# Fused local and coarse attention with a soft mixture of experts on one core: scores of both heads of a pair in one product, new layouts and a new order

## The chip, the cores and the metric

The kernel runs on one core of one Trainium2 chip. The metric is device time in microseconds (us) of one execution. Before the change three runs took 379.61, 382.04 and 382.05 us, median 382.04. The profile is of one more execution, which took 383.51 us, with a span of 381.7 us from its first to its last instruction.

## What is computed

Attention with 8 batches, 8 heads, 576 positions and 64 features a head, followed by a soft mixture of 8 experts with 4 slots each. All is 32-bit.

```python
q_d, k_d, v_d = (mean of 4 neighbouring positions of q, k, v)   # 144 positions
out_up = repeat(softmax(0.125 * q_d @ k_d.T) @ v_d, 4)
mask = abs(pos[:, None] - pos[None, :]) < 4                     # a band 7 wide
out_local = softmax(where(mask, 0.125 * q @ k.T, -1e9)) @ v
x = (out_up + out_local), as (4608 tokens, 512)
logits = x @ phi                                                # (4608, 32)
slot_input = softmax(logits, over tokens).T @ x                 # (32, 512)
slot_out[e] = relu(slot_input[e] @ w1[e]) @ w2[e]               # 512 -> 1024 -> 512
out = softmax(logits, over slots) @ slot_out
```

## The kernel before

x is never formed. The program holds instead, for each head, the product of v with that head's rows of phi, and gets the logits from attention weights times that product; the slot inputs come the same way, with the attention weights applied to the token weights first.

**Halves and steps.** The attention runs over 16 halves: a half is two pairs of heads (r = 0, 1) of one batch, four heads (k = 0 to 3). Two halves make a step, one batch. Two heads of a pair lie on partitions 0 to 63 and 64 to 127 (`h2`). The operations of a half, by their names in the order table: `lq` loads a pair's queries, keys and values in one DMA (888 KB); `pa`, `pb` (GpSimd, lines 145 and 151) add neighbours for the coarse means; `lv` loads values in another layout (640 KB); `sl` (line 173) makes the local scores, 24 queries by 30 keys a product, above a mask that two bf16 products (line 163) write first; `slm` to `sln` are their softmax; `ptt`, `pte` transpose the weights; `vf` (line 238) is v times phi; `sd`, `sr` (lines 275, 285) are the coarse scores (128 queries, and the last 16 of 144), `sde` their exponentials (ScalarE), `sdn` the division (GpSimd, lines 325 to 328); `td` transposes them; `loc` (372) and `plg` (381 to 388) add both parts to the logits of the step in PSUM. After the second half the step's softmax over tokens follows (`pl`, `lts`, `mx` to `dx`, `dtt`), and then for both halves `es` (405) and `ed` (415 to 422), which apply the attention weights to the token weights, `ede` to `ett`, and `so` (452), the product with v. The halves overlap: `es` of a step stands among the `sl` of the next.

**How the products lie in the array.** TensorE products name a tile of the array by `tile_position`. A score product takes 64 rows and a strip of 32 columns, so that eight of them lie beside each other; `es` takes tiles of 24 rows by 32 columns on the diagonal, four beside each other; `loc`, `plg`, `ed` and `so` take all 128 rows and a strip of 32 columns, four beside each other. The trace shows a 32-bit product as two weight loads and two matmuls (so 96 products of a half's `sl` are 192 of each); a transpose or a bf16 product is one of each.

**What sets the order.** Within the attention, every engine's order is written by hand in the string ORDER: all engines take their instructions in that order, SP its DMAs too. Loads of expert weights stand in it as `w:n` (512 KB each). The first 27 of 64 (NW) go into their own buffers during the attention. 24 more (NW2) go into memory that attention tiles give back, each as soon as its place is free, and the last 13 into places of used weights.

**After the attention** (the tail) come the slot inputs, the first layer (`a<-wt,sits`, line 639), the second (666), and the outputs (691 to 699), 24 of them, in an order by hand for TensorE and SP.

Of the kernel before, what the change touches and what calls it, by code (L numbers as in the profile page):

```python
# [11 lines left out]
F32 = mybir.dt.float32  # L12
# [30 lines left out]
NW = 27  # L43
NW2 = 24
NP_, ND, NQK, NV, NWK = 4, 4, 4, 2, 2

# [9 lines left out]
def body(ctx, tc, qkv_, vk, phi, w1, w2, cst, cstb, out):  # L56
# [27 lines left out]
    with ExitStack() as att:  # L84
        ld = att.enter_context(tc.tile_pool(name="ld", bufs=NQK))
        lv = att.enter_context(tc.tile_pool(name="lv", bufs=NV))
        per = att.enter_context(tc.tile_pool(name="per", bufs=1))
        wk = att.enter_context(tc.tile_pool(name="wk", bufs=NWK))
        w1k = att.enter_context(tc.tile_pool(name="w1k", bufs=1))
# [10 lines left out]
        ets = [per.tile([P, 4, 160], F32, name=f"et{i}") for i in range(2)]  # L100
        lgs = [per.tile([P, 152], F32, name=f"lg{i}") for i in range(2)]
        dts = [per.tile([P, 152], F32, name=f"d{i}") for i in range(1)]
# [9 lines left out]

        halves = [{} for _ in range(2 * B)]
        steps = [{"started": set()} for _ in range(B)]
        qts = {}

        def load_qk(i):
            b, pr = divmod(i, NPR)
            qts[i] = ld.tile([P, VO + KP], F32, name="qkv")
            sp.dma_start(out=qts[i], in_=qkv_[b, pr])  # L120

        def ops_half(h):
# [4 lines left out]
            e, pd, pk, pdr = es[h % NP_], pds[h % ND], pks[h % ND], pdrs[h % ND]  # L127
# [8 lines left out]
            for r in range(2):  # L136
                @at(f"lq{r}")
                def _(r=r):
                    load_qk(q[r])

                @at(f"pa{r}")
                def _(r=r):
                    t4 = qts[q[r]][:, 0:VO - 4].rearrange("p (t f) -> p t f", f=4)
                    t = hd[f"tmp{r}"] = w1k.tile([P, QP + 1 + SD, 2], F32, name="tmp")
                    pool.tensor_tensor(out=t, in0=t4[:, :, 0:2], in1=t4[:, :, 2:4], op=ALU.add)  # L145

                @at(f"pb{r}")
                def _(r=r):
                    t = hd[f"tmp{r}"]
                    hd[f"qd{r}"] = w1k.tile([P, QP + 1 + SD], F32, name=f"qd{r}")  # L150
                    pool.tensor_tensor(out=hd[f"qd{r}"], in0=t[:, :, 0], in1=t[:, :, 1], op=ALU.add)  # L151
# [72 lines left out]
            def _():  # L224
                hd["pt"] = wk.tile([P, NC, NG, QB], F32, name="pt")
# [5 lines left out]
            def _():  # L231
                vf = hd["vf"] = bank2("vf").rearrange("p a n -> p (a n)")
                for c0, c1 in ((0, 512), (512, KP)):
                    for r in range(2):
                        for h2 in range(2):
                            k = 2 * h2 + r
                            o = slice(64 * h2, 64 * h2 + 64)
                            pe.matmul(vf[32 * k:32 * k + 32, c0:c1], lhsT=phs[o, 2 * hf + r, :],  # L238
                                      rhs=qts[q[r]][o, VO + c0:VO + c1], start=True, stop=True,
                                      tile_position=(64 * h2, 32 * k), skip_group_check=True)  # L240
# [7 lines left out]
            def _():  # L248
                dve.tensor_reduce(out=vdps[h % 2][:, 0:SD], in_=hd["vf"][:, 4:4 + S].rearrange("p (t f) -> p t f", f=4),  # L249
# [13 lines left out]
            def _():  # L263
                hd["vr"] = wk.tile([P, SLOTS], F32, name="vr")
                dve.transpose(out=hd["vr"], in_=vdps[h % 2][:, P:160])


            @at("sd")
            def _():
                sd = hd["sd"] = bank2("sd")  # L270
                for r in range(2):
                    for h2 in range(2):
                        o = slice(64 * h2, 64 * h2 + 64)
                        qd = hd[f"qd{r}"]
                        pe.matmul(sd[:, h2, SD * r:SD * r + SD],  # L275
                                  lhsT=qd[o, 0:P], rhs=qd[o, QP + 1:], start=True, stop=True, tile_position=(64 * h2, 0), skip_group_check=True)

            @at("sr")
            def _():
                for r in range(2):  # L280
                    for h2 in range(2):
                        o = slice(64 * h2, 64 * h2 + 64)
                        qd = hd[f"qd{r}"]
                        k = 2 * h2 + r
                        pe.matmul(hd["sd"][32 * k:32 * k + 32, 0, 2 * SD:3 * SD],  # L285
                                  lhsT=qd[o, QP - 32:QP], rhs=qd[o, QP + 1:], start=True, stop=True, tile_position=(64 * h2, 32 * k), skip_group_check=True)
# [590 lines left out]
```

## Time and profile before

| | |
|---|---|
| Median of three runs | 382.04 us |
| Profiled execution, its span | 383.51 us, 381.7 us |
| TensorE matmuls: busy, share, number | 273.6 us, 72%, 9098 |
| TensorE weight loads: number | 9098 |
| VectorE, ScalarE, GpSimd busy | 147.7, 104.9, 160.0 us |
| Mean granted TensorE clock | 0.783 of 2.4 GHz |
| DMA | 84.25 MB, mean 221 GB/s |

How to read it: busy is the time in which an engine had an instruction under way. A wait is the idle time of an engine before an instruction, with what ended it; "issue" stands where the engine waited for nothing that the profile can name. The profile also counts DMA queues: q1 carries the program's own loads and stores, q8 carries instructions to the engines, in packets of 16 KB. An instruction is 64 bytes, so a packet holds 256; TensorE's two times 9098 instructions are 1.16 MB, which is what q8 moved. The text calls such a packet a block.

### The profile page before, as it was taken

The numbers are of one execution on the slowest core, as the hardware profiler recorded it, in microseconds if no ns is written. First come the engines' busy times: TensorE is split into PE (matmuls) and PEld (weight loads), VectorE is DVE, ScalarE is ACT, GpSimd is POOL, SyncE is SP. The second block draws the span as 40 slices with busy tenths as digits, with TensorE's granted clock in tenths as the row PEclk, the third lists the DMA queues.
The fourth block names the chain that finished last, engine by engine and source line by source line (L and its number), as shares of the span: only waits on it lengthen the run. The fifth ranks groups of instructions, "written<-read, shape, count | busy, mean of one in ns | idle before, by whom it ended". The sixth has DMA issues, their size and how long they took to land.

```text
span 381.7 us, 19650 instructions
## 1 busy us (share of the span) xinstructions
PE 273.6 (72%) x9098; PEld 199.8 (52%) x9098; DVE 147.7 (39%) x329; ACT 104.9 (27%) x333; POOL 160.0 (42%) x270
## 2 busy tenths in 40 slices
PE   0775695968487647785875688668795775999983
PEld 0534363845375537663763575447574664235552
DVE  1462632344334433452361534443480344001552
ACT  1222233222304140423141414140441411010442
POOL 3754827271627263636272625463742253100000
PEclk9986867596858885986596958875997855799997
DMA  7897536055903690289045900760272159999997
GB/s 271 324 330 300 191 149 271 6 214 206 379 8 115 247 413 32 99 327 377 6 136 184 373 6 10 258 261 5 72 299 109 52 203 320 411 409 409 385 371 289
DMA packets 20098, 84.25 MB, mean 221 GB/s; under 512 B 2224, under 2 KB 2608, under 8 KB 20016
## 3 DMA queue, kind: packets, MB, share of 16 engines
q1 hardware_dynamic: 20016, 82.99, 56.6%
q8 instruction: 71, 1.16, 1.2%
q14 instruction: 11, 0.09, 0.1%
HBM read 73.55 MB, written 9.44 MB: 217 GB/s over the span
## 4 chain that ended last, share of the span: by engine, by line
PE 69%; issue 23%; DVE 3%; DMA 2%; POOL 1%; ACT 0%; SPq 0%; ACTq 0%
PE ep L405 11%; PE sl L173 9%; PE vf L238 6%; PE a L639 4%; PE pt L220 4%; PE a L666 4%; PE so L452 4%; PE o L691 3%; PE sd L275 3%; PE td L335 2%; PE l L372 2%; PE ep L422 2%; DMA qkv<-qkv 2%; PE ep L415 2%; PE sl L163 2%
## 5 line engine op out<-in xcount | busy, mean ns | idle before, releaser
L173 PE MATMUL sl<-qkv 64*24 64x30 f32 x3072 | 34.2, 207 | 57.6 <-issue 51.3
L173 PEld LDWEIGHTS sl<-qkv 64*24 64x24 f32 x3072 | 29.8, 106 | 66.1 <-issue 58.9
L405 PE MATMUL ep<-e,dt 24*32 24x60 f32 x1536 | 44.2, 300 | 10.3 <-issue 9.2
L405 PEld LDWEIGHTS ep<-e,dt 24*32 24x32 f32 x1536 | 39.1, 166 | 12.9 <-issue 10.4
L183 DVE TENSOR_REDUCE nm<-sl 128x24 f32<-128x720 f32 x16 | 14.5, 908 | 79.8 <-PE sl L173 79.7
L145 POOL TENSOR_TENSOR tmp<-qkv 128x594 f32<-128x594 f32 x32 | 37.7, 1178 | 12.8 <-DMA qkv<-qkv 11.9
L195 ACT ACTIVATE e<-e 128x768 f32<-128x768 f32 x16 | 13.5, 846 | 69.2 <-DVE e L187 69.2
L325 POOL TENSOR_TENSOR pdr<-pdr,dd 128x144 f32<-128x144 f32 x16 | 6.8, 427 | 60.5 <-DVE dd L320 60.5
L309 ACT ACTIVATE xd<-sd,nd 128x144 f32<-128x144 f32 x64 | 23.5, 380 | 26.2 <-POOL nd L301 26.2
L440 POOL TENSOR_TENSOR et<-et,ed 128x576 f32<-128x576 f32 x16 | 19.2, 1212 | 26.6 <-ACT et L435 23.7
L238 PE MATMUL vf<-qkv,phs 64*32 64x512 f32 (+1 forms) x256 | 26.0, 520 | 1.4 <-issue 1.4
L151 POOL TENSOR_TENSOR qd<-tmp 128x297 f32<-128x297 f32 x32 | 21.8, 683 | 8.7 <-PE sd L285 7.6
L212 POOL TENSOR_TENSOR e<-e,den 128x720 f32<-128x720 f32 x16 | 22.5, 1406 | 2.5 <-DVE den L208 1.3
L452 PE MATMUL so<-v,ett 128*32 128x64 f32 x640 | 16.4, 260 | 8.8 <-issue 8.2
L227 ACT COPY pt<-pt 128x576 f32<-128x576 f32 x16 | 10.3, 646 | 45.0 <-PE pt L220 45.0
L187 DVE TENSOR_TENSOR e<-sl,nm 128x768 f32<-128x768 f32 x16 | 15.2, 952 | 15.2 <-PE ep L405 14.9
L249 DVE TENSOR_REDUCE vdp<-vf 128x144 f32<-128x576 f32 x16 | 12.1, 757 | 23.2 <-PE vf L238 23.1
L238 PEld LDWEIGHTS vf<-qkv,phs 64*32 64x32 f32 x256 | 9.1, 129 | 18.8 <-issue 18.5
L452 PEld LDWEIGHTS so<-v,ett 128*32 128x32 f32 x640 | 13.0, 133 | 10.5 <-issue 8.6
L639 PE MATMUL a<-wt,sits 128*32 128x512 f32 x128 | 16.8, 672 | 1.3 <-DVE sits L606 1.3
L220 PE MATMUL pt<-cs,e 128*128 128x128 f32 x96 | 17.6, 333 | 0.0
L445 DVE STREAM_TRANSPOSE ett<-et 128x640 f32<-128x640 f32 x16 | 13.0, 815 | 9.7 <-POOL et L440 9.6
(122 smaller groups left out, 536.6 us busy)
## 6 DMA issues: line engine op xcount, KB each, us to landing
wt<-w SPq DMA_DIRECT2D x64, 512.0 KB, 9.0
qkv<-qkv SPq DMA_DIRECT2D x32, 888.0 KB, 7.3
v<-vk SPq DMA_DIRECT2D x16, 640.0 KB, 4.4
out<-o SPq DMA_DIRECT2D x16, 432.0 KB, 4.2
out<-o SPq DMA_DIRECT2D x8, 288.0 KB, 4.6
cs<-cst SPq DMA_DIRECT2D x1, 208.0 KB, 2.4
cb<-cstb SPq DMA_DIRECT2D x1, 128.0 KB, 2.2
phs<-phi SPq DMA_DIRECT2D x1, 64.0 KB, 2.1
```

Source lines behind the costliest of these rows:

```text
L145: pool.tensor_tensor(out=t, in0=t4[:, :, 0:2], in1=t4[:, :, 2:4], op=ALU.add)
L151: pool.tensor_tensor(out=hd[f"qd{r}"], in0=t[:, :, 0], in1=t[:, :, 1], op=ALU.add)
L173: pe.matmul(s5[32 * g:32 * g + QB, h2, c, r, 1:31], lhsT=t[o, q0:q0 + QB], rhs=t[o, KO + s0 + 1:KO + s0 + 31], start=False, stop=True, til ...
L212: pool.tensor_tensor(out=e3[:, :, 1:31], in0=e3[:, :, 1:31], in1=hd["den"].unsqueeze(2).broadcast_to([P, 24, 30]), op=ALU.mult)
L220: pe.transpose(pt.rearrange("p a n -> p (a n)")[:, o:o + P], e[:, c].rearrange("p k u -> p (k u)"), ident)
L238: pe.matmul(vf[32 * k:32 * k + 32, c0:c1], lhsT=phs[o, 2 * hf + r, :], rhs=qts[q[r]][o, VO + c0:VO + c1], start=True, stop=True, tile_posi ...
L309: act.activation(xd[:, k], hd["sd"][:, k // 2, SD * (k % 2):SD * (k % 2) + SD], AF.Exp, scale=SCALE_D, bias=nd[:, k:k + 1], accum_out=dd[: ...
L405: pe.matmul(ep[32 * g:32 * g + 32, 2 * h2:2 * h2 + 2, QB * c + 1:QB * c + 31], lhsT=st["dt"][o, c, :], rhs=e[o, c, 2 * h2:2 * h2 + 2, 1:31 ...
L440: pool.tensor_tensor(out=x4, in0=x4, in1=hd["ed"].unsqueeze(3).broadcast_to([P, 4, XG, 4]), op=ALU.add)
L452: pe.matmul(so[32 * k:32 * k + 32, :], lhsT=hd["ett"][:, k, kb, :], rhs=hd["v"][:, kb, k, :], start=kb == 0, stop=kb == NK - 1, tile_posit ...
L639: pe.matmul(hp[o:o + 32, :], lhsT=sits[:, kc, :], rhs=wt[(1, e + x, kc)][:, 512 * f:512 * f + 512], start=kc == 0, stop=kc == NPR - 1, til ...
L666: pe.matmul(soq[u][32 * g:32 * g + 32, :], lhsT=hts[e // 4][:, e % 4, 2 * g + f, :], rhs=w[:, g], start=(e, f) == (0, 0), stop=(e, f) == ( ...
```

## The change

The scores of both heads of a pair become one product. Queries lie with the two heads' features interleaved over 128 partitions; the keys of head 0 go to even partitions of one block of columns, those of head 1 to odd partitions of a second block, and the other half of each block is zero (set once; the three buffers `qk0` to `qk2` are kept). One product of 128 rows then gives 24 queries by 2 x 30 keys. The coarse scores do the same (128 x 2 x 144), and their sums of neighbours now also run over the zero blocks. phi lies as a block-diagonal matrix, so that one product of 64 columns gives both heads of a pair. `es` multiplies tiles of 64 by 64, with a token weight matrix that is masked to be block-diagonal (`dtm`, GpSimd). `plg` takes all four groups of positions in one product. The logits are completed in PSUM: `lrp` adds the coarse part, each column four times, by a product; the sum stays in PSUM and is read from there, and is copied (`ktr`) for the end, where it is transposed at once.

`sdn` moves from GpSimd to ScalarE (five multiplications of 128x144), half of the `pb` from GpSimd to VectorE. A pair's loads become four DMAs (304, two of 146 and 292 KB, the same bytes in sum). Three buffers for queries and keys and two for values take the place of four for all; 31 expert weight tiles are loaded during the attention, not 27, and 19 go into given-back memory, not 24. Memory pools stand in another order, and ORDER is new.

```diff
-NW = 27
-NW2 = 24
-NP_, ND, NQK, NV, NWK = 4, 4, 4, 2, 2
+NW = 31
+NW2 = 19
+NQK, NVT, NP_, ND, NV, NE_ = 3, 2, 4, 4, 2, 1
...
-                    load_qk(q[r])
+                    t = qkt[q[r]] = qks[n % NQK]
+                    sp.dma_start(out=t[:, 0:QW], in_=qt[b, pr])
+                    for h2 in range(2):
+                        sp.dma_start(out=t[h2::2, QW + KP * h2:QW + KP * h2 + KP], in_=kt[b, pr, h2])
+
+                @at(f"lt{r}")
+                def _(r=r):
+                    hd[f"vt{r}"] = lt_.tile([P, KP], F32, name="vt")
+                    sp.dma_start(out=hd[f"vt{r}"], in_=vt[b, 2 * hf + r])
...
-                    t = hd[f"tmp{r}"] = w1k.tile([P, QP + 1 + SD, 2], F32, name="tmp")
-                    pool.tensor_tensor(out=t, in0=t4[:, :, 0:2], in1=t4[:, :, 2:4], op=ALU.add)
+                    t = hd[f"tmp{r}"] = w0.tile([P, 2, QK // 4], F32, name="tmp")
+                    pool.tensor_tensor(out=t.rearrange("p f t -> p t f"), in0=t4[:, :, 0:2], in1=t4[:, :, 2:4],
+                                       op=ALU.add)
...
-                    pool.tensor_tensor(out=hd[f"qd{r}"], in0=t[:, :, 0], in1=t[:, :, 1], op=ALU.add)
+                    (dve if r else pool).tensor_tensor(out=hd[f"qd{r}"], in0=t[:, 0], in1=t[:, 1], op=ALU.add)
...
-                            for h2 in range(2):
-                                o = slice(64 * h2, 64 * h2 + 64)
-                                pe.matmul(s5[32 * g:32 * g + QB, h2, c, r, 1:31], lhsT=t[o, q0:q0 + QB],
-                                          rhs=t[o, KO + s0 + 1:KO + s0 + 31], start=False, stop=True,
-                                          tile_position=(64 * h2, 32 * g), skip_group_check=True)
+                            pe.matmul(s5[32 * g:32 * g + QB, r, c, :, 1:31], lhsT=t[:, q0:q0 + QB],
+                                      rhs=kk[:, :, s0 + 1:s0 + 31], start=False, stop=True,
+                                      tile_position=(0, 32 * g), skip_group_check=True)
...
-                        for h2 in range(2):
-                            k = 2 * h2 + r
-                            o = slice(64 * h2, 64 * h2 + 64)
-                            pe.matmul(vf[32 * k:32 * k + 32, c0:c1], lhsT=phs[o, 2 * hf + r, :],
+                        pe.matmul(vf[64 * r:64 * r + 64, c0:c1], lhsT=phs[:, 2 * hf + r, :], rhs=hd[f"vt{r}"][:, c0:c1],
...
+                    o = win(hd["sd"], 552 * r, 184, 2, SD)
+                    pe.matmul(o, lhsT=hd[f"qd{r}"][:, 0:P], rhs=kd(r), start=True, stop=True, skip_group_check=True)
...
+                for j in (2, 0, 1, 3, 4):
+                    o = pdr[:, 0:SD] if j == 2 else pd[:, j - j // 3, 0:SD]
+                    act.mul(o, o, hd["dd"][:, j:j + 1])
+
+            @at("pkc")
+            def _():
+                pool.tensor_copy(out=pk[:, :, 0:16], in_=pd[:, :, P:SD])
...
+                for c in range(NC):
+                    for r in range(2):
+                        for w in range(2):
+                            o = slice(64 * w, 64 * w + 64)
+                            x = ep[o, r, 0:2 * KW].rearrange("p (h n) -> p h n", h=2)[:, :, QB * c + 1:QB * c + 31]
+                            pe.matmul(x, lhsT=dtb[o, c, :], rhs=e[o, c, 2 * r:2 * r + 2, 1:31], start=c == 0, stop=True,
+                                      tile_position=(64 * w, 64 * w), skip_group_check=True)
...
+            @at("lrp")
+            def _():
+                for g in range(NG):
+                    pe.matmul(st["l"][32 * g:32 * g + 32, 0:TG].rearrange("p (x f) -> p x f", f=4), lhsT=i32,
...
+                pool.tensor_tensor(out=dtb.rearrange("p c (x s) -> p c x s", x=2),
```

Two places show what stands where. First TensorE, where the token weights of the second step are used: from a half's scores on. A name such as e_93 is one of the four buffers of a half's local weights. Before:

```order
L163 MATMUL sl<-cb 128x384
L173 MATMUL sl<-qkv 24x30 x96
L405 MATMUL ep<-e_93,dt 32x2x30 x48
L544 MATMUL drp<-cs,dpx 128x32
L405 MATMUL ep<-e_94,dt 32x2x30 x48
L415 MATMUL ep<-pd_97,dpt 32x2x36 x3
```

After the change, at the same kind of place:

```order
L177 MATMUL sl<-cb 128x384
L187 MATMUL sl<-qk_98 24x2x30 x24
L187 MATMUL sl<-qk_97 24x2x30 x24
L407 MATMUL ep<-e_103,dtb 64x2x30 x24
L414 MATMUL ep<-pd_107,dpt 32x144 x4
L418 MATMUL ep<-pdr_111,drt 32x36 x16
L247 MATMUL vf<-vt,phs 64x512 x2
```

A half's scores go from 96 products to 48, `es` from 48 to 24; only one half's `es` stands behind the scores, and its `ed` follows at once. Second SP, whose queue issues every load, in the middle of the attention (with buffer numbers). Before:

```order
L120 DMA qkv_965<-qkv 128x1776
L82 DMA wt_1237<-w1 128x1024
L82 DMA wt_1239<-w1 128x1024
L120 DMA qkv_1241<-qkv 128x1776
L156 DMA v_1409<-vk 128x1280
```

After the change:

```order
L170 DMA v_1757<-vk 128x1280
L145 DMA qk0_97<-qt 128x608
L147 DMA qk0_97<-kt 64x584 x2
L81 DMA wt_1787<-w1 128x1024
L152 DMA vt_1789<-vt 128x584
L81 DMA wt_1942<-w1 128x1024
L152 DMA vt_1944<-vt 128x584
L145 DMA qk1_98<-qt 128x608
```

The loads are smaller, and values, queries and keys, and weights alternate. Counted as the trace counts (two weight loads and two matmuls for a 32-bit product), the attention's matmuls go from 8448 to 5328 and those after it stay at 650, each with a weight load: per half `sl` from 192 to 96, `es` from 96 to 48, `ed` from 52 to 40, `vf` from 16 to 8, `sd` from 8 to 4, `plg` from 48 to 20, `td` from 9 to 6, and `lrp` adds 8 a step.

## Rows read from the trace of the kernel before

**Rows 1.** Waits of TensorE, 42 to 272.6 us: total us, times, longest.

```profile
PE sl L173 <- issue: 42.8, 16, 5.2
...
PE ep L422 <- issue: 1.1, 2, 0.6
```

**Rows 2.** The page's DMA queues: packets, MB, share of 16 engines.

```profile
q8 instruction: 71, 1.16, 1.2%
```

**Rows 3.** Timeline, TensorE: start, us, what, number; idle before in brackets.

```profile
121.05 1.45 PE L173 MATMUL sl<-qkv 64*24 64x30 f32 x151
127.14 0.66 PE L173 MATMUL sl<-qkv 64*24 64x30 f32 x41 [4.64 <-issue]
...
138.37 1.01 PE L173 MATMUL sl<-qkv 64*24 64x30 f32 x99
```

**Rows 4.** DMA queues, 128.5 to 141.5 us.

```profile
q1 hardware_dynamic: 897, 4.56, 88.2%
q8 instruction: 2, 0.03, 0.9%
```

**Rows 5.** DMA queues, 346.7 to 366 us.

```profile
q1 hardware_dynamic: 2447, 7.52, 98.7%
q8 instruction: 3, 0.05, 1.0%
```

**Rows 6.** DMA queues, 145 to 158.5 us.

```profile
q8 instruction: 4, 0.07, 2.1%
```

**Rows 7.** Windows: stretch, its us, busy us by engine, granted clock, DMA share, GB/s.

```profile
42.00:272.60 230.60, 163.89 (x6269) 129.72 (x6267) 91.73 (x203) 65.73 (x220) 113.23 (x191) 0.75 0.46 177
119.90:158.50 38.60, 26.39 (x1072) 21.51 (x1068) 15.64 (x36) 11.17 (x38) 18.87 (x32) 0.78 0.51 200
126.90:130.30 3.40, 3.16 (x87) 2.71 (x86) 2.15 (x4) 0.00 (x0) 0.20 (x1) 0.50 0.15 33
140.60:154.20 13.60, 9.13 (x383) 8.33 (x383) 3.06 (x5) 1.59 (x3) 4.07 (x8) 0.50 0.25 98
321.80:381.70 59.90, 50.12 (x648) 24.63 (x646) 18.19 (x46) 12.82 (x28) 1.90 (x2) 0.90 0.96 380
```

**Rows 8.** DMA queues, 42 to 272.6 us.

```profile
q8 instruction: 49, 0.80, 1.4%
```

**Rows 9.** Timeline, TensorE, within one step: start, us, what, number.

```profile
134.75 0.76 PE L275 MATMUL sd<-qd 64*128 64x144 f32 x8
135.44 0.45 PE L285 MATMUL sd<-qd 64*32 64x144 f32 x8
...
149.65 2.62 PE L405 MATMUL ep<-e,dt 24*32 24x60 f32 x96
152.20 0.46 PE L415 MATMUL ep<-pd,dpt 128*32 128x72 f32 x8
...
152.68 0.71 PE L422 MATMUL ep<-pdr,drt 128*32 128x36 f32 x32
153.18 0.45 PE L415 MATMUL ep<-pd,dpt 128*32 128x72 f32 x8
```

**Rows 10.** Groups by line, GpSimd and ScalarE: busy us, mean ns, idle before.

```profile
L145 POOL TENSOR_TENSOR tmp<-qkv 128x594 f32<-128x594 f32 x32 | 37.7, 1178 | 12.8 <-DMA qkv<-qkv 11.9
...
L151 POOL TENSOR_TENSOR qd<-tmp 128x297 f32<-128x297 f32 x32 | 21.8, 683 | 8.7 <-PE sd L285 7.6
...
L328 POOL TENSOR_TENSOR pd<-xd,dd 128x512 f32<-128x512 f32 x16 | 16.7, 1041 | 0.0
...
L431 ACT ACTIVATE ed<-ep 128x144 f32<-128x144 f32 x16 | 4.7, 296 | 29.2 <-PE ep L422 29.2
```

**Rows 11.** Chain that ended last, in order of time: start, us, what.

```profile
2.58 7.47 DMA qkv<-qkv
10.09 2.08 PE sl L173 x143
...
320.18 1.34 PE so L452 x40
```

More of the change, by code (lines that the diff above doesn't have):

```diff
@@ L100, in body @@
[L100 to L102 removed]
+        pk = per.tile([P, 4, 32], F32, name="pk")
+        vdps = [per.tile([P, 160], F32, name="vdp")]
+        dd_ = per.tile([P, NC, 32], F32, name="d")
+        dtb = per.tile([P, NC, 64], F32, name="dtb")
+        ets = [per.tile([P, 2, 2, 160], F32, name=f"et{i}") for i in range(NE_)]
@@ L566, in body @@
         with tc.manual_schedule(engines=None):
+            first = seq.index(next(x for x in seq if not isinstance(x, int)))
+            for x in seq[:first + 1]:
+                x()
             sp.dma_start(out=cb, in_=cstb)
@@ new lines @@
+pa1:4 dx:1 sdn:2 dp:1 lt1:4 sd:3 dtt:1 vft:3 dtm:1 ktr:1 td:2 trt:2 pkc:2 vfr:3 sr:3 lt0:4 dpx:1 tk:2 sla:3 sdm:3
+tke:2 drt:1 mxo:3 tde:2 es:0 slv:3 ndc:3 pb1:4 sln:3 sde:3 dre:1 vdr:3 loc:2 dpt:1 ls:1 ed:0 pa0:4 plg:2 vdt:3 eta:0
+vf:4 vde:3 ede:0 sda:3 etb:0 vft:4 w:4 lt1:5 ptt:3 lt0:5 sl:4 pte:3 sdr:3 pb0:4 ett:0 sdn:3 vfr:4 pa1:5 loc:3 w:5
+lq0:5 lq1:6 so:0 slm:4 lv:2 td:3 sa:0 vdr:4 pkc:3 sls:4 vdt:4 sd:4 vde:4 trt:3 sle:4 tk:3 sr:4 sdm:4 vf:5 tde:3
+tke:3 slr:4 ndc:4 plg:3 sde:4 pb1:5 es:1 sla:4 slv:4 pa0:5 vft:5 ed:1 vfr:5 pl:3 lrp:3 eta:1 sda:4 mx:3 sl:5 sln:4
@@ new lines @@
+ptt:5 sa:2 ndc:6 sl:7 ett:3 pte:5 sde:6 slv:6 pb1:7 sln:6 loc:5 w:10 lq0:8 slm:7 plg:5 vdr:6 vdt:6 sls:7 pa0:7 vde:6
+ptt:6 pl:5 pte:6 so:3 sle:7 lrp:5 sda:6 sa:3 lv:5 lq1:9 vf:7 pb0:7 mx:5 sdr:6 mxp:5 sdn:6 slr:7 pa1:8 mxb:5 sd:7
+w:11 lt1:8 mxr:5 ktr:5 vft:7 dx:5 al:5 td:6 dp:5 dtt:5 pkc:6 dpx:5 trt:6 sr:7 vfr:7 dtm:5 tk:6 drt:5 tke:6 loc:6
+sdm:7 tde:6 sla:7 mxo:7 es:4 slv:7 ndc:7 pb1:8 sln:7 sde:7 dre:5 vdr:7 dpt:5 ls:5 plg:6 ed:4 pa0:8 vdt:7 vde:7 eta:4
+ptt:7 w:12 lt0:8 ede:4 sl:8 sda:7 pte:7 etb:4 sdr:7 sdn:7 loc:7 pb0:8 lq0:9 lq1:10 ett:4 td:7 slm:8 pkc:7 sd:8 pa1:9
@@ new lines @@
+trt:7 sls:8 tk:7 tde:7 sr:8 so:4 tke:7 sdm:8 sle:8 w:13 lv:6 plg:7 sa:4 ndc:8 pl:7 vf:8 slr:8 sde:8 vft:8 lt1:9
+lrp:7 sla:8 lt0:9 es:5 mx:7 slv:8 ktr:7 pb1:9 sda:8 sln:8 ed:5 sdr:8 mxp:7 vfr:8 sdn:8 mxb:7 sl:9 mxr:7 vdr:8 pa0:9
+eta:5 trt:8 ede:5 dx:7 slm:9 w:14 lq0:10 vdt:8 ptt:8 vde:8 al:7 pkc:8 lq1:11 td:8 pb0:9 dp:7 pte:8 sls:9 tk:8 tke:8
+etb:5 loc:8 tde:8 dtt:7 sd:9 dpt:7 ls:7 sle:9 dtm:7 ett:5 plg:8 pa1:10 slr:9 sr:9 so:5 sdm:9 w:15 lv:7 es:6 dpx:7
+sa:5 pb1:10 ndc:9 sla:9 sde:9 mxo:9 drt:7 slv:9 pa0:10 dre:7 vf:9 vft:9 w:16 lt1:10 ed:6 sln:9 eta:6 sl:10 vfr:9
@@ new lines @@
+dpt:9 al:9 slr:11 plg:10 dtm:9 sr:11 ls:9 dpx:9 sdm:11 vf:11 mxo:11 sla:11 slv:11 ndc:11 pb1:12 drt:9 sln:11 sde:11
+es:8 w:19 lt1:12 dre:9 vft:11 pa0:12 vfr:11 ed:8 vdr:11 eta:8 ptt:11 ede:8 vdt:11 sda:11 sl:12 vde:11 etb:8 sdr:11
+pte:11 sdn:11 pb0:12 loc:11 slm:12 w:20 lq0:13 lq1:14 es:9 pkc:11 ett:8 pa1:13 sls:12 lt0:12 td:11 ed:9 trt:11
+sle:12 sd:12 eta:9 slr:12 ede:9 tk:11 tde:11 sr:12 etb:9 so:8 sdm:12 tke:11 w:21 lv:10 plg:11 sa:8 sla:12 ett:9
+ndc:12 pl:11 vf:12 sde:12 slv:12 pb1:13 sln:12 lt1:13 so:9 vft:12 lt0:13 lrp:11 w:22 lv:11 sl:13 mx:11 ktr:11 sa:9
@@ new lines @@
+sle:14 lv:12 ptt:13 sa:10 pte:13 es:11 slr:14 ndc:14 sde:14 pb1:15 sla:14 loc:13 slv:14 pa0:15 trt:13 ed:11 plg:13
+eta:11 vf:14 ede:11 sda:14 sln:14 sdr:14 sdn:14 vft:14 w:25 lt1:15 sl:15 pb0:15 trt:14 vfr:14 ptt:14 pkc:14 slm:15
+etb:11 vdt:14 sd:15 vde:14 pte:14 vdr:14 sls:15 pl:13 w:26 lt0:15 sr:15 lrp:13 sdm:15 sle:15 td:14 mx:13 tk:14
+ktr:13 ndc:15 ett:11 tke:14 sde:15 mxp:13 slr:15 mxb:13 vf:15 mxr:13 sla:15 mxo:15 slv:15 dx:13 sda:15 so:11 sln:15
+tde:14 sdr:15 dp:13 loc:14 sdn:15 sa:11 w:27 lv:13 dtt:13 plg:14 vft:15 dtm:13 al:13 ptt:15 vfr:15 pkc:15 td:15
```

397 lines of the change are left out of this document (177 added, 220 removed).

## The prediction

> **What bounds the kernel now.** I read the waits of TensorE first, over six steps (42 to 272.6 us). All nine of their rows name "issue" and together 66.5 us, from 42.8 us at `sl` down to 1.1 us [rows 1]: TensorE waits for no engine and no load, yet it idles 11.1 us a step. What it lacks shows in the timeline. A half's scores run 151 matmuls at some 10 ns each and then stand still for 4.64 us, amid one unchanged loop [rows 3]. The DMA queues tell the rest. Queue q8 brings instructions in blocks of 256, which is 128 matmuls with their weight loads, 71 blocks in all [rows 2]. Where loads keep the DMA engines busy, two blocks begin in 13.0 us and three in 19.3 us, so one each 6.5 us [rows 4, 5]; where no load runs, four in 13.5 us, one each 3.4 us [rows 6]. Over the six steps DMA is busy 0.46 of 230.6 us [rows 7]: 106 / 6.5 = 16 blocks, and the other 125 / 3.4 = 37 blocks, 53 in all, where 49 came [rows 8]. So arrival of code accounts for 93% of the time of a step (38.4 us), and TensorE's own work, 163.9 us busy or 27.3 a step [rows 7], fits in beneath it.
>
> The Trainium skill ("Runtime: NRT & Kernel Launch", Instruction fetch mechanics) also has blocks of 256 instructions, but calls the cost of crossing one mostly hidden. This trace shows 11.1 us a step that isn't hidden; by that rule the waits would have another cause, which is the third rival below.
>
> **What the change takes away: instructions.** The attention's matmuls fall from 8448 to 5328, a step's from 1056 to 666, its blocks from 8.25 to 5.2. A step's loads are 4 x 888 KB, 2 x 640 KB and 4.2 x 512 KB (24 weight loads stand spread over some 11.5 halves of the new order), 7.15 MB; at the 390 GB/s of rows 5 that is 18.3 us, in which 18.3 / 6.5 = 2.8 blocks come. The other 2.4 blocks come in quiet time, at 3.4 us or at TensorE's own pace, whichever is slower.
>
> **TensorE's own pace.** Term by term, for a half:
> - Scores: 192 matmuls at 1.01 us / 99 = 10.2 ns [rows 3], 1.96 us. Now 96 of 60 columns in four strips. No row has this shape; the nearest is `es`, also 60 columns and four tiles side by side, 2.55 us for 96, which is 26.6 ns at a granted clock of 0.5 [rows 7, 9], hence 13.3 at full clock: 1.28 to 2.55 us. I take 1.7, since most of `sl` runs at full clock. Less 0.3.
> - `es`: 48 in place of 96, but two tiles side by side, not four, so the same columns in sequence: 2.55 us again at the low clock, half at the high one. No change.
> - `sd`: eight matmuls in pairs of row halves took 0.69 us, start to start [rows 9]. Now four, twice as wide, with no partner: 1.38 us. Plus 0.7.
> - `vf`, `ed`: as many columns per strip. `plg` and `td` shrink, `lrp` is new; below 0.3 us either way, taken as minus 0.2.
>
> The zeros thus cost what the fewer instructions save: plus 0.2 us a half, 27.7 us a step at the clock as it is now. That clock is the second unknown. In the step from 119.9 us, 12.3 of 26.4 busy us lie in two stretches at 0.5, that is 1.2 GHz [rows 7]: one begins after the stall of rows 3, the other holds a stall, both `es` and `ed`. At 2.4 GHz throughout, the 12.3 would be 6.2 and the step's work 20.3 us. Both stalls should shorten, and a tile of 64x64 keeps more of the array at work than 24x32, so I take a point between, 24 us; ends 20.3 and 27.7.
>
> **The step and the sum.** 24 / 5.2 = 4.6 us a block. The step is 18.3 + 2.4 x 4.6 = 29.3 us (27.7 to 31.1 by the clock). The other unknown is the delay of a block behind the smaller loads: if none is delayed, TensorE's work alone is left, at least 20.3 us; if all are, 5.2 x 6.5 = 33.8. I take the rates as they are, since the bytes are the same. Of the 7% that the count falls short of now I keep 3%, as part of the step is no longer starved. Eight steps: 8 x 29.3 x 1.03 = 241 us (now 10.1 to 321.5, 311 us [rows 11]).
>
> Start: `sl` waited until 10.1 us for two pairs and three constants, 2176 KB in 7.5 us [rows 11]; now 1550 KB stand ahead of it, at that rate 2.1 us less, and as the zero blocks must be set first I take 1.9: 8.2. Tail: 381.7 - 321.5 = 60.2 us. TensorE is busy for 50.1 of 59.9 us and DMA for 0.96 [rows 7]; TensorE's work there is the same, 33 late weight loads in place of 37 give DMA 5 us of air, but the slot softmax now starts only after the attention, under the first layer. I leave it at 60.2. Outside the span lie 383.5 - 381.7 = 1.8 us. Sum: 8.2 + 241 + 60.2 + 1.8 = 311; the profiled execution is 1.5 us above the median of the runs, so **310 us** in their terms.
>
> Edits at nothing: `sdn` on ScalarE is 10 x 0.296 = 3.0 us a step on 11.2; half the `pb` goes to VectorE (15.6 now). GpSimd has 18.9 [rows 7]: `pa` grows by 888/594, 4 x 0.58 = 2.3; `pb` 2 x 1.02 for 4 x 0.68, less 0.7; `sdn` leaves, less 2 x 1.04 and more; `dtm` and `pkc` add about 1.4 [rows 10]: 19 or less. All lie under a step of 29 us. If that cover goes, GpSimd is first, at 65%. SP issues four loads for one, and has time for it.
>
> **The rivals.**
> 1. *Code arrives in time and the clock stays up.* Smaller loads, spread wider, delay a block less; fewer stalls keep 2.4 GHz. For it: 3.4 us a block in quiet time is below 3.9 that TensorE needs. Against it: over 60% of a step is now DMA time. A step of 20.3 us and some 3.7 of stalls, 24: 8 x 24 x 1.03 + 70 = 268 us.
> 2. *Other engines bind.* GpSimd at 65%, ScalarE at 50%, and one place for the logits in PSUM, which now must last until `dx` and `ktr` have read it before the next step's `loc` may write. TensorE would show waits for ScalarE or GpSimd, of which it now has none [rows 1]. Some 4 us a step: 33.3, or 343 us.
> 3. *The waits do not hang on the number of instructions.* Then they stay, 11.1 us, on 27.7 of work: 38.8 a step, no change, 382. Against it: rows 3 to 6.
> 4. *Slower: products of 128 rows in strips do not overlap.* The overlap of two row halves is given up; if the four strips ran one after another too, a score matmul would cost 4 x 26.6 = 106 ns at 1.2 GHz, 96 of them 10.2 us. In place of 1.7 that makes a step's work 24 + 17 = 41 us, more than code needs to arrive: 8 x 41 x 1.03 + 70 = 408 us. It decides where the step passes 37.8 us, at 8.6 us for a half's scores, 90 ns a matmul. Against it: `ed` has such matmuls, 128 rows and 32 columns, with 36 columns of data; 32 took 0.50 us, start to start, 15.6 ns each in the stretch at 1.2 GHz [rows 7, 9], which makes 26 ns for 60 columns.
>
> The Trainium skill ("TensorE: Matmul & The Clock Gate", Why this matters for your kernels) advises to put products of few rows into distinct row groups, where they run concurrently; this change does the opposite, and rival 4 is the hard form of that advice. The trace agrees with it for `sd` (0.69 us for eight [rows 9]) and not for `sl`, where the array waits for code.
>
> **How the numbers follow.** Forecast 0.50 (295 to 325, by clock and block delay), rival 1 0.20, rival 2 0.20, rival 3 0.05, rival 4 0.03, and 0.02 for a time below rival 1. For 8 in 10 the range must reach well into rivals 1 and 2: 272 to 345. A change under about 1% can't be told from none here. Faster by over 1%: 0.50 + 0.20 + 0.20 + 0.02 = 0.92; within 1%: rival 3, 0.05; slower: rival 4, 0.03.
>
> **What would show it.** Blocks: 71 becomes about 47. TensorE's "issue" waits in the steps fall from 11.1 us to about 4 or 5 a step; if they stay, rival 3. A half's 96 score matmuls in 1.3 to 2.6 us; 5 or more is rival 4. Mean granted clock of the steps above 0.75, about 0.85; 0.95 and more with a step near 24 us is rival 1. Waits of TensorE for ScalarE or GpSimd that sum to 3 us a step or more are rival 2. The tail within 3 us of 60. What would make the prediction wrong above all is the delay of blocks behind loads, as no run has yet had these sizes, and the clock under `es` in its new shape.

## The result, and the profile after

The changed kernel takes 306.29 us, the median of four executions (301.35 to 308.56), beside 382.05 us for the kernel before on the same chip (four executions, 379.61 to 385.52). The ratio is 0.796, with a 95% interval from 0.781 to 0.811. The profiled execution took 307.06 us, its span is 305.3 us. All ratios leave out the slow executions, those more than 1.5% above the fastest of their kernel (so 306.29 / 382.05 is not quite the one given), and of `a_no_loads` further down, whose profiled execution ran at 1.2 GHz nearly throughout and took 358.1 us where the others took 269 to 273, only the trace is used and not that time.

Nearly all of the gain lies in the attention. It runs from the first `sl` at 9.5 us to the last `so` at 245.1, 235.6 us; before it was 311.4. The start and the tail (60.2 us) changed by less than 1 us each. The page of the changed kernel has first the engines (busy us, share of the span, instructions), then the granted clock in 40 slices, the code queue as in [rows 2], and the chain that ended last:

```profile
PE 236.4 (77%) x5978; PEld 166.9 (55%) x5978; DVE 160.5 (53%) x328; ACT 131.2 (43%) x421; POOL 156.2 (51%) x182
...
PEclk9999986998879999979999999999979659999996
...
q8 instruction: 47, 0.77, 1.0%
...
PE 62%; issue 13%; DMA 6%; DVE 5%; SPq 5%; POOL 4%; ACT 3%; POOLq 0%; DVEq 0%
```

Code is down from 71 blocks to 47. In the chain "issue" stands at 13%; loads and the queue that issues them (DMA, SPq) make up 11%.

Here and below a **step** is a sixth of the time from the start of the 4th half's `sl` to that of the 16th, six steps in each kernel: 42.2 to 273.7 us before, 38.6 us a step; 38.8 to 205.9 after, 27.85. The waits of TensorE in these six steps (total us, times, longest), to set beside [rows 1]:

```profile
PE sl L187 <- issue: 11.6, 7, 3.2
PE l L372 <- issue: 5.5, 3, 2.7
PE l L382 <- issue: 3.6, 1, 3.6
PE vf L247 <- DMA vt<-vt: 2.2, 2, 1.3
PE ep L418 <- issue: 2.2, 1, 2.2
PE so L448 <- issue: 1.6, 1, 1.6
PE ep L407 <- issue: 1.4, 1, 1.4
PE drp L547 <- POOL nd L304: 1.3, 1, 1.3
PE mxb L497 <- DVE nd L490: 1.2, 2, 0.8
```

All rows with "issue" sum to 25.9 us, 4.3 a step, where there were 11.1. Waits for other engines and loads, of which there were none, sum to 6.4 us, 1.1 a step; the largest is for the value loads (`vt`). The windows view (stretch, its us; busy us of PE, PEld, DVE, ACT, POOL; granted clock, DMA share, GB/s) has the six steps and the tail:

```profile
38.80:205.90 167.10, 134.58 (x3979) 104.09 (x3980) 99.88 (x203) 89.82 (x308) 113.69 (x130) 0.95 0.73 250
...
245.10:305.30 60.20, 50.52 (x651) 25.10 (x650) 23.90 (x51) 14.27 (x29) 7.36 (x4) 0.90 0.89 350
```

TensorE is busy for 134.58 / 6 = 22.4 us a step, 27.5 before (164.79 us in its six steps), and the granted clock rose from 0.75 [rows 7] to 0.95. So a step lost 10.7 us: 6.8 of waits for code and 5.0 of TensorE's busy time, less 1.1 of new waits. The busy time fell with the clock and not with the work: at full clock the new work is 21.2 us a step (`a_no_loads2` below), and the prediction's estimate of the old was 20.3. The timeline of TensorE within one step (start, us, what, number, idle before) shows the new shapes, beside [rows 3] and [rows 9]:

```profile
97.31 1.46 PE L187 MATMUL sl<-qk 128*24 128x60 f32 x96
98.59 0.44 PE L372 MATMUL l<-pt,vw 128*32 128x24 f32 x29
...
105.11 1.22 PE L287 MATMUL sd<-qd 128*128 128x288 f32 x4
106.17 0.60 PE L337 MATMUL td<-cs,pd 128*128 128x128 f32 x4
...
108.14 1.61 PE L407 MATMUL ep<-e,dtb 64*64 64x60 f32 x48
109.68 0.43 PE L382 MATMUL l<-pdt,vd 128*32 128x128 f32 x8
...
112.89 0.45 PE L418 MATMUL ep<-pdr,drt 128*32 128x36 f32 x26 [2.22 <-issue]
```

A half's 96 score matmuls take 1.28 us start to start, the 48 of `es` 1.54, the four of `sd` 1.06. The last row is a stall of the old kind, smaller: a dense stretch of short products has used up its code, and TensorE stands for 2.22 us among unchanged products.

That these waits are for code can be read from where they fall. Two places of the kernel before, in the same view:

```profile
61.33 1.37 PE L173 MATMUL sl<-qkv 64*24 64x30 f32 x128 [1.30 <-issue]
66.15 0.40 PE L173 MATMUL sl<-qkv 64*24 64x30 f32 x20 [3.46 <-issue]
...
81.57 1.26 PE L173 MATMUL sl<-qkv 64*24 64x30 f32 x128 [0.42 <-issue]
87.76 0.30 PE L173 MATMUL sl<-qkv 64*24 64x30 f32 x4 [4.93 <-issue]
```

Between one wait and the next lie 128 matmuls, with their weight loads exactly one block. The times of the packets of q8 in the traces say the same: of the waits named "issue" of 1 us or more in the six steps, all 23 before and all 12 after ended 1.2 to 1.6 us after such a packet had landed.

### The profile page after: what moved, and what is told of

The parts are those of the page before. It is cut to its first block, busy times and chain, and to the rows that moved or that the text cites. A ratio compares the mean times of both kernels' runs of the same rounds, so it can differ in the third digit from the quotient of the medians.

```text
span 305.3 us, 13591 instructions
## 1 busy us (share of the span) xinstructions
PE 236.4 (77%) x5978; PEld 166.9 (55%) x5978; DVE 160.5 (53%) x328; ACT 131.2 (43%) x421; POOL 156.2 (51%) x182
## 4 chain that ended last, share of the span: by engine, by line
PE 62%; issue 13%; DMA 6%; DVE 5%; SPq 5%; POOL 4%; ACT 3%; POOLq 0%; DVEq 0%
PE ep L407 7%; PE sl L187 7%; PE a L646 5%; PE sd L287 5%; PE vf L247 5%; DMA vt<-vt 5%; PE a L673 5%; PE o L698 4%; PE pt L232 3%; SPq L147 3%; PE so L448 3%; PE l L372 2%; PE l L382 2%; PE sl L177 2%; PE sd L293 2%
## 5 line engine op out<-in xcount | busy, mean ns | idle before, releaser
L158 POOL TENSOR_TENSOR tmp<-qk 128x888 f32<-128x888 f32 x32 | 57.5, 1798 | 7.6 <-DMA qk<-kt 6.5
L187 PE MATMUL sl<-qk 128*24 128x60 f32 x1536 | 26.6, 222 | 15.0 <-issue 12.4
L436 POOL TENSOR_TENSOR et<-et,x 128x576 f32<-128x576 f32 x16 | 19.5, 1216 | 30.8 <-ACT x L425 24.0
L187 PEld LDWEIGHTS sl<-qk 128*24 128x24 f32 x1536 | 22.8, 106 | 21.9 <-issue 21.2
L312 ACT ACTIVATE pd<-sd,nd 128x144 f32<-128x144 f32 x64 | 24.0, 386 | 21.4 <-POOL nd L304 21.4
L407 PE MATMUL ep<-e,dtb 64*64 64x60 f32 x768 | 28.5, 230 | 2.3 <-issue 2.3
L407 PEld LDWEIGHTS ep<-e,dtb 64*64 64x64 f32 x768 | 26.1, 144 | 6.7 <-issue 5.8
L247 PE MATMUL vf<-vt,phs 128*64 128x512 f32 (+1 forms) x128 | 21.3, 457 | 5.3 <-DMA vt<-vt 5.3
L287 PE MATMUL sd<-qd 128*128 128x288 f32 x64 | 22.0, 471 | 1.7 <-POOL qd L165 1.7
L327 ACT ACTIVATE pd<-pd,dd 128x144 f32<-128x144 f32 x64 | 21.2, 407 | 0.0
```

The source lines that it names most:

```text
L158: pool.tensor_tensor(out=t.rearrange("p f t -> p t f"), in0=t4[:, :, 0:2], in1=t4[:, :, 2:4], op=ALU.add)
L187: pe.matmul(s5[32 * g:32 * g + QB, r, c, :, 1:31], lhsT=t[:, q0:q0 + QB], rhs=kk[:, :, s0 + 1:s0 + 31], start=False, stop=True, tile_posit ...
L247: pe.matmul(vf[64 * r:64 * r + 64, c0:c1], lhsT=phs[:, 2 * hf + r, :], rhs=hd[f"vt{r}"][:, c0:c1], start=True, stop=True, tile_position=(0 ...
L287: pe.matmul(o, lhsT=hd[f"qd{r}"][:, 0:P], rhs=kd(r), start=True, stop=True, skip_group_check=True)
L312: act.activation(o, hd["sd"][:, 184 * j:184 * j + SD], AF.Exp, scale=SCALE_D, bias=nd[:, j:j + 1], accum_out=dd[:, j:j + 1])
L327: act.mul(o, o, hd["dd"][:, j:j + 1])
```

## The experiments

The theory of the prediction: code comes in blocks of 256 instructions, more slowly where loads run, and its arrival sets the time of a step. The rivals: the work taken away counts, not its code; other engines or loads bind; the tiles' shape holds the clock. In lines of variants the line numbers are those of the variant, some up to 11 higher.

**Fewer products alone, before (`b_one_head`).** Half of the score products go, nothing else.

```diff
-                            for h2 in range(2):
+                            for h2 in range(1):
```

> The kernel before, with the local score products of the second head of each pair left out (half of sl: 96 matmuls a half in place of 192; the output is not the reference's). If late code sets the step: 1.5 blocks of instructions a step fewer, all of them in quiet time at 3.4 us, 5.1 us a step, about 339 us in all. If TensorE's own work sets it and the waits have another cause: 96 matmuls of 10.2 ns less a half, 2 us a step, about 366 us.

Measured 339.68 us (ratio 0.876, 0.868 to 0.883), 59 blocks. The kernel before takes 385.8 us on that chip, so 46 us went with 12 blocks, 3.8 us each, where code was to give 43 (339 from 382) and the work alone 16. That the time itself comes within 1 us of 339 is luck.

**More code alone, after (`a_more_code`).** 48 idle products of one column behind a half's scores, 12 more blocks in all.

```diff
+                for x in range(48):
+                    g = x % 4
+                    pe.matmul(sl[32 * g:32 * g + 32, 1, 400:401], lhsT=ident[:, 0:32], rhs=ident[:, 0:1],
+                              start=False, stop=True, tile_position=(0, 32 * g), skip_group_check=True)
```

> The changed kernel with 48 idle products added after the scores of each half (one column each, into unused columns): 96 matmuls and 96 weight loads more, 1.5 blocks a step. If late code sets the step: 1.5 x 3.4 = 5.1 us a step more, about 347 us. If TensorE's work sets it: 96 x 10.2 ns a half, 2 us a step, about 322 us. If other engines set it: 306 to 312 us.

Measured 358.52 us (0.924, 0.914 to 0.933), more than any theory expected. The waits of TensorE over six steps (total us, times, longest):

```profile
PE sl L192 <- issue: 14.6, 6, 4.4
PE sl L187 <- issue: 7.6, 5, 3.0
```

The longest row stands at the idle products themselves (line 192), and all "issue" rows sum to 47.4 us, 7.9 a step. The windows view of the same stretch:

```profile
44.20:253.10 208.90, 159.83 (x5131) 125.50 (x5131) 98.43 (x204) 89.60 (x307) 111.92 (x129) 0.84 0.60 195
```

The clock fell back from 0.95 to 0.84, TensorE is busy 26.6 us a step for 22.4, and the step is 34.8 us, 7.0 more for 1.5 blocks. By the ratios to before it is (0.924 - 0.796) x 385.8 us, the median of before on that chip, some 49 us for 12 blocks, 4.1 us a block; with 0.787, which the changed kernel gave once more (`a_again` below), it is 53 us and 4.4. The idle products' own time is not that much: the trace has 92 of their matmuls in 1.49 us, so 96 a half make some 25 us in all.

**The old shape of `es`, after (`a_old_es`),** and the changed kernel once more beside it (`a_again`).

```diff
...
-                            o = slice(64 * w, 64 * w + 64)
...
-                            pe.matmul(x, lhsT=dtb[o, c, :], rhs=e[o, c, 2 * r:2 * r + 2, 1:31], start=c == 0, stop=True,
-                                      tile_position=(64 * w, 64 * w), skip_group_check=True)
...
+                            o = slice(32 * g, 32 * g + QB)
...
+                            pe.matmul(x, lhsT=st["dt"][o, c, :], rhs=e[o, c, 2 * r:2 * r + 2, 1:31], start=c == 0, stop=True,
+                                      tile_position=(32 * g, 32 * g), skip_group_check=True)
```

> The changed kernel itself, unchanged, beside the three others of this group, so that small differences can be read on one chip. Expected: 306 us within 1%, 47 blocks of instructions, attention about 236 us.

> The changed kernel with es on tiles of 24 by 32 again, four side by side, as before the change: 96 matmuls a half for 48, and the same products in sum. Theory (code): 96 matmuls a step more are 0.75 of a block, 12 halves-pairs' worth make 6 blocks, 53 for 47; in the run with 48 more idle products a half 0.75 block a step cost 7.0 us, of which the products' own time is a part; so 3 to 6 us a step, 25 to 45 us, time 332 to 350. If besides the tile's shape is what holds the clock up, es falls to a granted clock of 0.5, 2.55 us for its 96 matmuls, and the mean clock of the attention goes from 0.95 towards 0.85. Rival: the clock stays above 0.9 wherever code is on time and falls only after waits for code, whatever the shape; then es takes some 1.3 us between its waits. Rival: the time doesn't hang on the number of instructions: 306.

Measured 304.68 us for `a_again` (0.787, 0.781 to 0.793; 47 blocks, attention 232.7) and 329.55 for `a_old_es` (0.850, 0.842 to 0.858; 53 blocks): 24.9 us for six blocks, again 4.1 us each, and just below the foot of what was expected. The timeline of TensorE in `a_old_es`, at a place at full clock and at one with a stall:

```profile
46.54 1.46 PE L407 MATMUL ep<-e,dt 24*32 24x60 f32 x96
47.93 0.60 PE L372 MATMUL l<-pt,vw 128*32 128x24 f32 x47
...
82.95 0.45 PE L418 MATMUL ep<-pdr,drt 128*32 128x36 f32 x10 [4.17 <-issue]
...
84.08 2.62 PE L187 MATMUL sl<-qk 128*24 128x60 f32 x96
86.63 1.94 PE L407 MATMUL ep<-e,dt 24*32 24x60 f32 x96
```

At the first place the 96 matmuls of the old shape take 1.39 us start to start, less than the 48 of the new (1.54). So the new `es` saves no array time; it saves code. At the second the scores take 2.55 us, twice their 1.28. The windows view has the granted clock (the third number from the end) of both places:

```profile
80.90:87.70 6.80, 4.75 (x152) 3.88 (x156) 0.94 (x2) 2.36 (x7) 2.92 (x4) 0.50 0.02 6
46.50:50.00 3.50, 2.82 (x195) 2.59 (x195) 1.83 (x7) 2.85 (x13) 2.77 (x4) 1.00 0.93 356
```

The first place ran at 1.00, so the old shape does not by itself pull the clock down there. Half clock is seen from 80.9 us on, inside the wait of 4.17 us that ends at 82.95.

**Fewer loads (`b_no_w`, `a_no_w`).** All but one of the early expert weight loads go.

```diff
+        if 0 < n < NW:
+            wt[wq[n]] = wt[wq[0]]
+            return
```

> The kernel before with 26 of the 27 expert weight loads of the attention left out (the first layer reads one tile in their place; the output is not the reference's). Instructions and work of TensorE are unchanged. If loads delay blocks of code: 2.6 MB a step less, one block a step comes in 3.4 us in place of 6.5, some 3.2 us a step over five and a half steps, attention 17 us shorter, about 364 us. If loads do not matter to TensorE, which waits for none of them: 382 us. The tail may shift a little, as the late loads find free places; the attention's own length decides.

> The changed kernel with 30 of the 31 expert weight loads of the attention left out, in the same way. If late code still holds part of the step: blocks come sooner, 2 us a step, about 290 us, and TensorE's waits by issue fall from 4 us a step to 2 or less. If other engines, or loads of values, hold it: 306 us within 2 us.

Measured 377.09 us (0.974, 0.967 to 0.980) and 299.08 us (0.769, 0.761 to 0.776). Both gained, half of what was expected. Steps: 36.9 for 38.6, and 25.25 for 27.85, with "issue" at 2.7 us a step for 4.3. Both times carry a side effect: late weight loads found their places free and were issued early, 13 at some 19 to 33 us in `b_no_w` and 11 at 27 to 38 us in `a_no_w`; in `a_no_w` a half waited 11.2 us for its keys behind them, ahead of the six steps. So loads do delay code, but the price of a quiet block had to be wrong; hence the next pair.

**Nearly no loads (`b_no_loads`, `a_no_loads`, `a_no_loads2`).** Beyond the edit above, queries, keys and values are loaded once for each buffer and used again (here the edit of `b_no_loads`).

```diff
+            if i >= NQK:
+                qts[i] = qts[i % NQK]
+                return
...
+                if h >= NV:
+                    hd["v"] = halves[h % NV]["v"]
+                    return
```

> The kernel before, with nearly all loads of the attention left out: queries, keys and values are loaded for the first two halves only and used again by all others, and 26 of 27 expert weight tiles are replaced by the first. All engines keep their instructions. Theory (loads delay code, and code is the bound): all 8.25 blocks of a step come at the quiet rate, 3.4 us each, 28 us, and TensorE's own work is 27.3: the step falls from 38.6 to 28 to 31 us, the attention from 311 to 230 to 250. Rival (blocks come at their own pace whatever the loads do): the step stays near 38. Since the kernel without its weight loads lost only 6 of 311 us, a point between is possible: then the 3.4 us were too short a price for a quiet block.

> The changed kernel with the same left out: queries, keys and values are loaded only until each buffer is filled once and used again from there, and 30 of 31 expert weight tiles are replaced by the first. Theory: 5.2 blocks a step at the quiet 3.4 us are 17.7 us, less than TensorE's work of 20 to 22, so code is in time: the waits named issue fall from 4.0 to under 1 us a step, the step from 27.9 to 22 to 24 us, the attention from 236 to 180 to 195; TensorE itself is then the bound, and the clock stays at 1.0. Rival (blocks come at their own pace, or TensorE's waits for code have another cause): issue stays at 3 to 4 us a step and the step at 25 or more. Rival (GpSimd, 18.4 us of work a step, binds as soon as code doesn't): TensorE waits for GpSimd, by 2 us a step or more.

> The changed kernel with nearly all loads of the attention left out, as in a_no_loads, profiled once more, since the execution profiled there ran at 1.2 GHz nearly throughout (granted clock 0.567) and took 358 us, where its other three took 269 to 273. Expected: 270 us, step 23 to 24 us, clock 1.0 in the attention. Theory (code in time when no load runs): issue waits under 1 us a step. Rival (a quiet block costs 3.9 us rather than 3.4, as the kernel before showed without its loads, so dense stretches still outrun it): issue 1 to 2 us a step, 5.2 blocks in 20 us at the least. Rival (GpSimd binds): TensorE waits for it by 2 us a step or more.

Measured 351.32 us before (0.908, 0.903 to 0.913) and 271.75 after (0.709, 0.700 to 0.718, `a_no_loads2`; `a_no_loads` gave 0.700, 0.695 to 0.705). Six steps of `b_no_loads` in the windows view:

```profile
44.00:238.90 194.90, 153.45 (x6311) 121.66 (x6312) 92.96 (x206) 66.15 (x224) 113.91 (x193) 0.83 0.02 4
```

And its longest waits of TensorE there:

```profile
PE sl L182 <- issue: 22.4, 12, 2.7
PE ep L414 <- issue: 8.4, 5, 2.2
```

Without a load under way (DMA 0.02) it still waits for code, 39.5 us in all rows, 6.6 a step, and its step is 32.5 us, beyond the far end of what was expected: 49 blocks in 194.9 us, 3.98 us each. The changed kernel (`a_no_loads2`), six steps:

```profile
34.70:173.50 138.80, 127.44 (x3980) 98.33 (x3983) 98.44 (x204) 89.87 (x308) 112.49 (x130) 1.00 0.02 7
```

Its longest waits of TensorE there:

```profile
PE ep L418 <- issue: 2.1, 3, 1.1
PE sl L198 <- issue: 1.8, 2, 1.0
```

Its step is 23.1 us, and all "issue" rows sum to 8.5 us, 1.4 a step, a little more than the theory had and what a quiet block of 3.9 us gives. TensorE, busy for 21.2 us a step at full clock, is the bound there; GpSimd, at 112.5 of 138.8 us, still does not bind. The execution of `a_no_loads` at 1.2 GHz, six steps:

```profile
41.80:233.10 191.30, 189.29 (x3980) 135.52 (x3982) 98.22 (x201) 91.10 (x309) 113.73 (x131) 0.55 0.01 3
```

TensorE is slow enough here never to outrun its code: busy for 189.29 of 191.3 us, with 0.5 us of "issue".

With 3.98 us for a quiet block the six steps of before give the price of one under loads, if the DMA share is taken as a share of the time: 0.46 of 231.5 us are 106.5, the other 125 hold 31.4 blocks, the remaining 17.6 of 49 cost 6.05 us each. These two prices against the blocks that came in six steps of the others:

| kernel | six steps, DMA share | blocks by the prices | blocks counted |
|---|---|---|---|
| `b_no_w` | 221.4 us, 0.36 | 48.8 | 49 |
| `b_one_head` | 195.9 us, 0.54 | 40.1 | 41 |
| changed | 167.1 us, 0.73 | 31.5 | 32 |
| `a_no_w` | 151.5 us, 0.63 | 29.9 | 31 |
| `a_old_es` | 183.1 us, 0.68 | 35.3 | 37 |
| `a_more_code` | 208.9 us, 0.60 | 41.7 | 40 |
| `a_no_loads2` | 138.8 us, 0.02 | 34.6 | 32 |

In six rows the count is within 2 of what could come, as it should be where code is the bound, and four times it is up to 1.7 above, so the two prices hold to some 5%. The last row took 2.6 fewer than could have come; there TensorE's work is the bound.

**Two new waits (`a_lt_first`, `a_mxp_tt`, `a_both`).** The value loads stand in SP's queue behind loads that wait for a buffer; and a 128x4 instruction on VectorE (line 490) takes some 1 us.

```diff
-... vf:6 sle:6 pa1:7 eta:3 vft:6 w:9 lt1:7 td:5 lt0:7 sd:6 ...
+... vf:6 lt1:7 lt0:7 sle:6 pa1:7 eta:3 vft:6 w:9 td:5 sd:6 ...
```

```diff
-                dve.tensor_scalar(out=nd5[:, 0:4], in0=mask4, scalar1=st["nk"], scalar2=None, op0=ALU.mult)
+                dve.tensor_tensor(out=nd5[:, 0:4], in0=mask4, in1=st["nk"].broadcast_to([P, 4]), op=ALU.mult)
```

> The changed kernel with the loads of a half's values (vt) moved in the hand-written order: they are issued right after the vf of the half before has read the buffers, ahead of the loads of queries and keys that wait for a score buffer. In the trace vf waits 3.2 us for vt in six steps, and the chain that ended last has 5% of the span in vt's transfers and 5% in SP's queue, together about 30 us. Theory (the loads' place costs what the chain shows): the waits for vt vanish and the time falls by 3 to 6 us, to 300 to 303. Rival (code is the deeper bound): what the loads give back the waits for code take, 305 to 307. By the chain's shares alone it would be up to 30 us: 276.

> The changed kernel with the masked maximum (line 490, 128x4 on VectorE) written as a product of two tensors in place of a product with a per-partition scalar. In the trace this small instruction takes 190 to 1506 ns, 1003 at the median, where its size asks for some 200. Theory (the form's): it falls to about 0.2 us, and with it the wait of TensorE on it, 1.2 us in six steps: the time falls by 1 to 4 us, 302 to 305. Rival (VectorE is held by what GpSimd does at that time): it still takes about 1 us, and the time stays at 306.

> The changed kernel with both edits of the runs a_lt_first and a_mxp_tt: values loaded right behind the vf of the half before, and the masked maximum as a product of two tensors. Alone, the first gave no gain (306.7 beside 304.7 us) and the second 1.7 us at most (302.9), both within the spread of their runs. Theory (code is the bound, so what one wait gives back the next wait for code takes): 301 to 306 us, not to be told from the changed kernel. Rival (the two waits hide each other, and both gone give their sum of some 4 us and more): below 299.

Measured 306.66 us (six executions, 296.45 to 314.93) for the first, 302.94 (0.780, 0.773 to 0.786) for the second, 304.23 (0.784, 0.780 to 0.788) for both, beside 304.68 (0.787, 0.781 to 0.793). None can be told from the changed kernel. In the six steps of `a_lt_first` no wait for `vt` is left (2.9 us in `a_again`), but "issue" is 28.2 us in place of 23.0, so the next wait for code took what the load gave back, as far as one profile each can say. Whether these edits are worth 1% stays open; no version that surely beats the changed kernel was found.

## Why the prediction was right

310 was predicted, within 272 to 345, and 306.3 came. The mechanism held; some terms were off and in part cancelled, and that much of the closeness is luck.

- **Blocks:** 47 predicted, 47 came. This is the term that carried the forecast, and `b_one_head`, `a_old_es` and `a_more_code` show it as cause: they move the number of instructions alone, or nearly so, and the time follows by 3.8 to 4.4 us a block. The Trainium skill ("Runtime: NRT & Kernel Launch", Instruction fetch mechanics) calls the cost of crossing a block mostly hidden; here 48 idle products a half cost some 50 us, so the measurement decides against it.
- **Price of a block:** 6.5 us under loads and 3.4 in quiet were read from three short stretches [rows 4 to 6]. Over whole steps it is 6.05 and 3.98. Four blocks in one short stretch gave nearly the shortest gap, not the mean: in the trace of before, the 22 gaps between blocks in the six steps in which nearly no load ran (other queues busy under a tenth of the gap) are 3.25 to 4.51 us, 3.7 on average. This is the term that was mis-sized, and one reason why `b_no_w`, `a_no_w` and `b_no_loads` gained less than expected. It did not enter the sum, which took TensorE's own 4.6 us for a quiet block.
- **Time of the loads:** 18.3 us a step at 390 GB/s was predicted. DMA was busy for 0.73 x 27.85 = 20.3 us: in its busy time it moved 250 / 0.73 = 342 GB/s, in the old layout 177 / 0.46 = 385 [rows 7]. That the smaller pieces cost these 11% is likely, but no run tried it alone. Here two terms cancelled: 18.3 us under loads and 2.4 x 4.6 = 11.0 without were predicted, 20.3 and 7.5 came. By the price of 6.05, 3.4 of the 5.2 blocks came under loads, and the other 1.8 took 4.1 us each.
- **TensorE's work:** 24 us taken, between 20.3 and 27.7; 22.4 came, at a clock of 0.95 and not 0.85. At full clock it is 21.2. The reason given for a higher clock, that 64x64 tiles keep more of the array at work, is not borne out: the old tiles ran at 1.00 too, in the first place shown of `a_old_es`. A half's scores took 1.28 us (1.7 taken, 1.28 its lower end), `sd` 1.06 (1.38), `es` 1.54 where half of 2.55 was its lower end.
- **Step and ends:** six steps took 167.1 us for 6 x 29.3 = 175.8, while the ends of the attention (first three halves and all behind the 16th half's start) took 68.5, where two steps and the 3% give 65.6. Together 235.6 for 241.
- **Issue waits:** 4 to 5 us a step predicted, 4.3 came.
- **Edits at nothing:** GpSimd has 113.69 / 6 = 18.9 us a step (19 or less), ScalarE 15.0. Its `sdn` takes 407 ns each in place of the 296 taken, so plus 4 us a step and not 3; hidden all the same.
- **Start and tail:** the first `sl` came at 9.5 us, not 8.2: it waits for keys, and SP issues nine transfers one after another, some 0.6 us each, until 6.2 us. The tail is 60.2 us for 60.2. The start in the timeline of TensorE:

```profile
6.09 0.82 PE L177 MATMUL sl<-cb 128*128 128x384 bf16 x2 [6.09 <-DMA cb<-cstb]
9.46 2.61 PE L187 MATMUL sl<-qk 128*24 128x60 f32 x96 [2.55 <-DMA qk<-kt]
```

The first scores wait 2.55 us for `kt`, whose load is the last of those nine.

The rivals: the first (code in time, clock up, a step of 24 us) came halfway, by its clock alone; `a_no_loads2` shows that it is about what the kernel does where no load delays code, at 23.1 us a step. The second (other engines bind) is 1.1 us a step of waits, not 4. The third falls with `b_one_head`. The fourth asked for 90 ns a score matmul and more; 1.28 us / 96 is 13.3 ns.

## What to carry to other kernels

Where TensorE waits for "issue" amid an unchanged loop, count instructions before columns: here 256 instructions cost some 4 us, 16 ns each, whether they did work or not, so a product that multiplies zeros but stands for two was the cheaper one. Take the price of a block from whole steps, not from the shortest gap, and test it by a few idle instructions. A wait that is removed beneath such a bound can come back as a wait for code.

## What the runs showed that was not expected

**A tiny instruction that takes long.** Line 490 on VectorE in the changed kernel, by the view of one line (duration min/median/max in ns):

```profile
L490 DVE TENSOR_SCALAR nd<-cs,nk x8: 190/1003/1506, 46.4 to 226.0; 128x4 f32<-128x4 f32 x8
```

The same line in `a_mxp_tt`, in its other form:

```profile
L490 DVE TENSOR_TENSOR nd<-cs,nk x8: 120/258/1332, 41.9 to 228.9; 128x4 f32<-128x4 f32 x8
```

Both forms can take 0.2 us or well over 1 us, and in `a_both` the second form has a median of 512 ns. So the form alone is not the cause. The traces point to GpSimd: the instruction is held until GpSimd's own is done. The slowest of the eight in the changed kernel, in the timelines of GpSimd and VectorE:

```profile
182.22 1.89 POOL L158 TENSOR_TENSOR tmp<-qk 128x888 f32<-128x888 f32 x1
182.62 1.51 DVE L490 TENSOR_SCALAR nd<-cs,nk 128x4 f32<-128x4 f32 x1
```

Of the 40 in the five runs with this line in either form (the changed kernel, `a_again`, `a_lt_first`, `a_mxp_tt`, `a_both`), 22 took over 0.3 us. Each of these began while an addition or multiplication of two tensors ran on GpSimd and ended within 0.1 us of its end. Of the other 18, which took 0.12 to 0.23 us, 16 began while GpSimd was idle and two within the last 0.1 us of such an instruction. No run took the work off GpSimd to try it.

**The clock after a wait.** The six steps of the changed kernel had a granted clock of 1.00 without loads (1.4 us of "issue" a step), 0.95 as it is (4.3), and 0.84 with 12 more blocks (7.9). In the changed kernel's six steps four stretches ran at half clock, and each began within 1.3 us of the end of one of the four longest waits for code (2.65 to 3.56 us). What runs in such a stretch takes twice as long: in `a_old_es` 2.55 us for 1.28 at the scores after the stall. How much of this lengthens the step is not shown, since the next block arrives meanwhile. Nor are waits the only way to half clock: the execution of `a_no_loads` at 1.2 GHz had 0.5 us of them, and why it ran so is open.
